# Edge messages summed by node in float32, one step later, with the message's add behind the ranks

## The chip, the cores and the metric

One core of a Trainium2 chip runs the kernel. The metric is the time of the whole program on the device in microseconds (us); the time before is the median of three runs. The profile is of one further execution. Engines are named as in the profile: PE is TensorE's matmul, PEld its weight load, DVE is VectorE, ACT ScalarE, POOL GpSimd, SP SyncE. POOL issues the indirect DMAs (gathers and scatters) in this kernel, SP most of the others.

## The reference

A message-passing step on a graph with N = 12500 nodes, E = 800000 edges, 64 features a node and 16 an edge:

```python
def reference(x, e_attr, src, dst, w_msg, w_upd):
    N, D = x.shape
    m_in = jnp.concatenate([x[src], x[dst], e_attr], axis=-1)
    msg = _silu(m_in @ w_msg)
    agg = _segment_sum(msg, dst, N)
    return _silu(jnp.concatenate([x, agg], axis=-1) @ w_upd)
```

All floating-point inputs are float32. `src` and `dst` are random, so the edges come in no order.

## The kernel before

**Tables.** At the start, x is multiplied once by the part of `w_msg` for the source (table `A_d` in DRAM, one row a node) and once by the part for the destination (table `BW` on chip, by buckets). A message is then the sum of a gathered row of `A_d`, a row of `BW` picked by a one-hot product, and the edge's 16 features times their weights.

**Sorting on chip.** Nodes are cut into 128 buckets of 98. Edges are read in chunks of 8 tiles of 128, 782 chunks in all. For a chunk, `onehot` (L362) makes the one-hot of each edge's bucket, `sums` (L368 to 371) adds these over tiles in bfloat16, `count` (L379 to 381) turns them on TensorE into each edge's rank in its bucket, `ranks` (L386) takes the largest entry, `expand` (L395 to 399) spreads each edge's record into the slot of its rank, `move` (L407) multiplies by the one-hot and so brings the records to their buckets in PSUM, ScalarE copies them to `blk` (L409), `place` (L415, 416) advances the buckets' pointers and `scatter` (L420) writes the block to the store `st` in DRAM, as one indirect DMA on POOL.

**Work list.** A group of tiles of the store (48 or 24 in two short first stages with units of u = 1 and u = 2 tiles, then 64 with units of QU = 4) is formed over several steps: `fourth` and `middle` work out on VectorE and TensorE which tiles of which bucket are complete (matmuls into `ps1` and `ps2`, read by VectorE at L512 to 514, 521 and 522), SP loads them (L497), and `fifth` takes the edges' source indices `sidx` (L463) and local destinations `lo` from them.

**Messages.** A group is worked off in batches of 8 tiles (6 in the u = 2 stage). `gather` (L574) issues one indirect DMA on POOL a tile, from `A_d` into one of three buffers `g`. `onehot` (L579) makes the one-hot `q` of the local destinations, with the edge features beside it (L580); `transpose` turns it (L588, copied to `qt` at L591), `weights` picks the bucket's rows of `BW` (L567), `product` multiplies (L597). `message` adds the gathered rows on VectorE (L603) and applies SiLU on ScalarE (L604). `parts` (L612) splits the float32 message into three bfloat16 parts by two subtractions, `reduce` multiplies them by the one-hot and so sums by node (L623; in batches with u other than 4 in float32, L625), and `add` sums the three parts (L636) and adds the result to `ACC` (L638).

**Order.** The scheduler is off: each engine gets its instructions in the order of the program text. `period()` writes out one step. It takes a chunk through one stage each of `h`, `z`, `p`, `s`, and a batch through `q` (gather and one-hot), `t` (transposes and product) and `a` (message and reduce), so that several chunks and batches are under way. After the last chunk there are periods with a batch alone, and between them `Update.run` (L878 to 886) forms the output for buckets that are done. `ends` (L901) writes terminators behind each bucket's last record.

Of the kernel before, what the change touches and what calls it, by code (L numbers as in the profile page):

```python
# [43 lines left out]
def mpnn_kernel(tc, x, e_attr, src, dst, w_msg, w_upd, out):  # L44
# [22 lines left out]
    with es:  # L67
# [62 lines left out]
        sent = cp.tile([P, 32, R], F32, name="sent")  # L130
# [69 lines left out]
        def tables():  # L200

            ts = [Nodes(qp, "q" if b0 // 4 % 2 else "qt", b0) for b0 in range(0, NB, 4)]
# [127 lines left out]
        for k in range(P // 32):  # L330
            nc.sync.dma_start(st_t[D0:D0 + DUM, k * 32 * R:(k + 1) * 32 * R], sent[0:DUM].rearrange("p a b -> p (a b)"))
# [12 lines left out]
        qp = pool("qp", 3)  # L344
# [82 lines left out]
        class Group:  # L427
# [40 lines left out]
            def fourth(g):  # L468
# [15 lines left out]
                elif k == 1:  # L484
                    a1, v, new, e0, s, e, t1, cbc = g.wl
                    g.mat = mat = wp.tile([NBK, GT], F32, name="mat")
                    nc.vector.tensor_scalar(out=mat[:, 0:gu], in0=iof[:, 0:gu], scalar1=s, scalar2=None, op0=OP.is_ge)

                    nc.vector.tensor_tensor(out=t1, in0=t1, in1=s, op=OP.subtract)
                    nc.vector.tensor_tensor(out=a1, in0=e, in1=s, op=OP.subtract)  # L490
                    nc.vector.scalar_tensor_tensor(out=mat[:, 0:gu], in0=iof[:, 0:gu], scalar=e, in1=mat[:, 0:gu], op0=OP.is_lt, op1=OP.mult)
                    nc.vector.tensor_scalar(out=cbc, in0=t1, scalar1=float(g.u), scalar2=-float(D0), op0=OP.mult, op1=OP.add)
                    nc.vector.tensor_tensor(out=g.done_new, in0=g.done_old, in1=a1, op=OP.add)
                elif k < g.t0:
                    for u in range((k - 2) * g.nl, min(gu, (k - 1) * g.nl), 8):
                        for i, t in enumerate(regs(g.row, u, min(8, gu - u), ENG.SP, TOP - g.u)):
                            j = nc.sync.dma_start(g.rt[:, (u + i) * g.u:(u + i + 1) * g.u, :].rearrange("p a c -> p (a c)"),  # L497
                                                  st_t[ds(t, g.u), :].rearrange("t (q f) -> (t q) f", f=g.u * R))
                            tc.add_to_no_dep_group("units", j.ins)
                            if len(blocks) > g.blocks:  # L500
                                for b in blocks[g.blocks:]:
                                    tc.declare_no_dep(j.ins, b, reason=WHOLE)
                                tc.add_manual_dep(j.ins, blocks[g.blocks - 1].name, mybir.DependencyInfo(mybir.DependencyClass.Sync, mybir.DependencyReason.DATA), reason=WHOLE)

            def middle(g):

                gu = g.gu
                if g.k == 0:
                    a1, v, new, e0, s, e, t1, cbc = g.wl
                    ps = pp.tile([P, 512], F32, name="ps1", tag="pl")  # L510
                    nc.tensor.matmul(ps[:, 0:1], tri, new, start=True, stop=True)
                    nc.vector.tensor_tensor(out=e0, in0=ps[:, 0:1], in1=new, op=OP.add)  # L512
                    nc.vector.tensor_scalar(out=s, in0=ps[:, 0:1], scalar1=float(gu), scalar2=None, op0=OP.min)
                    nc.vector.tensor_scalar(out=e, in0=e0, scalar1=float(gu), scalar2=None, op0=OP.min)
                elif g.k == 1:
                    cbc, mat = g.wl[7], g.mat
                    ps2 = pp.tile([P, 512], F32, name="ps2", tag="pl")
                    nc.tensor.matmul(ps2[0:1, 0:gu], cbc, mat[:, 0:gu], start=True, stop=True)
                    nc.tensor.matmul(ps2[0:1, gu:2 * gu], b64, mat[:, 0:gu], start=True, stop=True)
                    g.row, g.rb = wp.tile([1, GT], I32, name="row"), rbp.tile([1, GT], I32, name="rb")  # L520
                    nc.vector.scalar_tensor_tensor(out=g.row[:, 0:gu], in0=ps2[0:1, 0:gu], scalar=float(D0), in1=iof[0:1, 0:g.gt:g.u], op0=OP.add, op1=OP.add)
                    nc.vector.tensor_copy(g.rb[:, 0:gu], ps2[0:1, gu:2 * gu])

        class Last(Group):
# [15 lines left out]
            def middle(g):  # L540
                if g.k == 0:
                    ps = pp.tile([P, 512], F32, name="ps3", tag="pl")
                    nc.tensor.matmul(ps[0:1, 0:g.gu], g.wl[:, 1:2], ident[:, g.b0:g.b0 + g.gu], start=True, stop=True)
                    g.row = wp.tile([1, GT], I32, name="row")
                    nc.vector.tensor_copy(g.row[:, 0:g.gu], ps[0:1, 0:g.gu])

        class Batch:
# [13 lines left out]
            def weights(t):  # L561

                t.w = None
                if t.grp.u == QU:
                    t.w = qp.tile([KQ, BT // QU, D], F32, name="w")
# [16 lines left out]
            def transpose(t, step):  # L582
# [6 lines left out]
                else:  # L589
                    t.qt = qp.tile([KQ, BT * P], F32, name="qt")  # L590
# [8 lines left out]
            def message(t):  # L599
                w = t.n * D  # L600
                t.msg = mp.tile([P, 3, BT * D], F32, name="msg")
                u_ = t.msg[:, 2, :]
                nc.vector.tensor_tensor(out=u_[:, 0:w], in0=t.pre[:, 0:w], in1=t.g.rearrange("p a b -> p (a b)")[:, 0:w], op=OP.add)  # L603
                nc.scalar.activation(t.msg[:, 0, 0:w], u_[:, 0:w], AF.Silu)  # L604

            def parts(t):

                t.split = t.grp.u == QU
                if t.split:
                    up = t.msg.bitcast(BF16).rearrange("p k (f two) -> p k f two", two=2)  # L610
                    for k in range(2):
                        nc.vector.tensor_tensor(out=t.msg[:, k + 1, :], in0=t.msg[:, k, :], in1=up[:, k, :, 1], op=OP.subtract)  # L612

            def reduce(t):
                t.ag = pag.tile([P, 512], F32, name="ag")
                w = 3 * D
                if t.split:
                    q = t.q.bitcast(BF16).rearrange("p i (k two) -> p i k two", two=2)[:, :, 0:BK, 1]
                    m = t.msg.bitcast(BF16).rearrange("p k (f two) -> p k f two", two=2)[:, :, :, 1]
                for i in range(t.n):  # L620
                    u, k = i // t.grp.u, i % t.grp.u
                    if t.split:
                        nc.tensor.matmul(t.ag[0:BK, u * w:(u + 1) * w].rearrange("p (k d) -> p k d", d=D), q[:, i, :], m[:, :, i * D:(i + 1) * D], start=(k == 0), stop=(k == t.grp.u - 1))  # L623
                    else:
                        nc.tensor.matmul(t.ag[0:BK, u * D:(u + 1) * D], t.q[:, i, 0:BK], t.msg[:, 0, i * D:(i + 1) * D], start=(k == 0), stop=(k == t.grp.u - 1))  # L625

            def add(t):
# [4 lines left out]
                s = t.ag[0:BK]  # L632
                if t.split:
                    nu = BT // QU
                    s = mp.tile([BK, nu * D], F32, name="sum")
                    nc.vector.tensor_reduce(out=s.rearrange("p (u d) -> p u d", d=D), in_=t.ag[0:BK, 0:nu * 3 * D].rearrange("p (u k d) -> p u d k", k=3, d=D), axis=AX.X, op=OP.add)  # L636
                for u, a in enumerate(t.at(ACCf, ENG.DVE)):
                    nc.vector.tensor_tensor(out=a, in0=s[:, u * D:(u + 1) * D], in1=a, op=OP.add)  # L638
# [4 lines left out]
        def period(chunk=None, batch=None, ptr_new=None):  # L643

            h, z, p, s = chunk, pipe["h"], pipe["z"], pipe["p"]
            q, t, a = batch, pipe["q"], pipe["t"]
            forms = [g for g in work["forming"] if not g.ready()]
            pipe.update(h=h, z=z, p=p, q=q, t=t)
            if z:
                z.count()  # L650
            if a:
                a.message()
            if t:
                t.transpose(0)
            if h:
                h.onehot()
            if t:
                t.weights()
                t.transpose(1)
            if q:  # L660
# [5 lines left out]
            if a:  # L666
                a.parts()
# [4 lines left out]
            if z:  # L672
                z.ranks()
            for g in forms:
# [5 lines left out]
            if a:  # L680
                a.reduce()
                a.add()
            if p:
                p.place(ptr_new)
            for g in forms:
                g.middle()
                g.fifth()
            if t:
                t.product()
            return a  # L690
# [205 lines left out]
        pe = cp.tile([NBK, P // 32], I32, name="pe")  # L896

        def ends(ptr):
            for k in range(P // 32):
                nc.vector.tensor_scalar(out=pe[:, k:k + 1], in0=ptr, scalar1=float(32 * k), scalar2=None, op0=OP.add)  # L900
                i = nc.gpsimd.indirect_dma_start(out=st, out_offset=bass.IndirectOffsetOnAxis(ap=pe[:, k:k + 1], axis=0),  # L901
                                                 in_=sent.rearrange("p a b -> p (a b)"), in_offset=None)
                tc.declare_no_dep(i.ins, group="units", reason=WHOLE)
# [11 lines left out]
        def last(b=None):  # L915

            if b and b.b0 in us:
                us[b.b0].load()
# [156 lines left out]
```

## Time and profile before

| what | before |
|---|---|
| median of 3 runs | 11522.06 us (11520.64 to 11545.6) |
| the profiled execution | 11522.43 us |
| its span, first to last instruction | 11520.6 us |
| mean granted TensorE clock | 0.817 |
| busy: PE, PEld | 8812.3, 6708.3 us (76%, 58%) |
| busy: DVE, ACT, POOL | 8786.3, 2487.4, 6874.6 us (76%, 22%, 60%) |
| DMA | 521.39 MB, mean 45 GB/s |

Busy time counts instructions at work; the gap between two DMA issues on POOL is not in it. In a row of a group stand line, engine, operation, output and inputs, then the count after x, the busy time and the mean of one in ns, and the idle time of the engine just before these instructions with what ended most of it. "remote" is a semaphore whose sender the profile can't name, "issue" a time in which the engine waited for nothing that the profile shows. In a row of waits stand engine, name and line of the waiting instruction, what released it, and total, count and longest wait.

### The profile page before, as it was taken

The page shows a single profiled execution, that of the slowest core. Times are in us where ns is not written, and L with a number is a line of the kernel's source. Part 1 is how long each engine was busy: PE and PEld are TensorE (multiplying, and loading weights), DVE is VectorE, ACT ScalarE, POOL GpSimd, SP SyncE. Part 2 cuts the span into 40 slices and gives each one's busy share as a digit, 9 for nine tenths or more (in the row PEclk, how much of TensorE's full clock was granted, in tenths as well). Part 3 has the DMA queues.
Part 4 walks back from the last instruction along what each step waited for, and adds up shares of the span by engine and source line. Part 5 has one row for each costly group of instructions (what it writes and reads, how often), then busy time and mean ns, then how long its engine had stood idle before and what let it go on. Part 6 is the DMA issues. An engine that isn't in the chain of part 4 may idle for free. (4 is left out here: it accounts for less than half of the span.)

```text
span 11520.6 us, 142616 instructions
## 1 busy us (share of the span) xinstructions
PE 8812.3 (76%) x43298; PEld 6708.3 (58%) x44060; DVE 8786.3 (76%) x18300; ACT 2487.4 (22%) x5785; POOL 6874.6 (60%) x7129
## 2 busy tenths in 40 slices
PE   7777777777777777777777777777777777777566
PEld 4555555555555555655655555565655565555466
DVE  8777777888888888878888888887888888887322
ACT  2111112222222222222222222222222222222111
POOL 2455556666666666666666666666666666666555
PEclk9888888888888888788888888888888888888555
DMA  2111111111111111111111111111111111111212
GB/s 64 39 43 46 41 44 49 44 47 46 44 47 44 48 43 47 47 44 47 44 47 44 46 47 44 47 44 47 47 43 47 45 46 47 43 46 41 44 36 39
DMA packets 661675, 521.39 MB, mean 45 GB/s; under 512 B 472583, under 2 KB 520135, under 8 KB 660903
## 3 DMA queue, kind: packets, MB, share of 16 engines
q0 software_dynamic: 252672, 378.89, 12.3%
q1 hardware_dynamic: 405527, 132.58, 5.2%
q8 instruction: 359, 5.88, 0.2%
q14 instruction: 413, 3.38, 0.1%
q10 hardware_dynamic: 2704, 0.66, 0.0%
HBM read 330.05 MB, written 181.46 MB: 44 GB/s over the span
## 5 line engine op out<-in xcount | busy, mean ns | idle before, releaser
L574 POOL DMA_INDIRECT g<-A_d,sidx x6322 | 6077.2, 961 | 3146.3 <-issue 1669.5
L407 PE MATMUL pl<-X,hf 128*128 128x427 f32 (+3 forms) x12512 | 3946.6, 463 | 637.9 <-issue 463.4
L407 PEld LDWEIGHTS pl<-X,hf 128*128 128x128 f32 x12512 | 2461.8, 203 | 1966.5 <-issue 1238.1
L399 DVE TENSOR_TENSOR X<-cb,rec 128x850 f32<-128x850 f32 (+3 forms) x3128 | 2379.7, 823 | 26.8
L597 PE MATMUL pre<-w,qt 114*128 114x64 f32 x10496 | 1725.2, 333 | 458.1 <-ACT qt L591 385.0
L597 PEld LDWEIGHTS pre<-w,qt 114*128 114x128 f32 x10496 | 1653.0, 247 | 507.1 <-ACT qt L591 421.3
L604 ACT ACTIVATE msg<-msg 128x512 f32<-128x512 f32 (+1 forms) x818 | 503.3, 615 | 5688.6 <-DVE msg L603 4660.0
L603 DVE TENSOR_TENSOR msg<-pre,g 128x512 f32<-128x512 f32 (+1 forms) x818 | 550.8, 673 | 1431.6 <-remote 1041.7
L420 POOL DMA_INDIRECT st<-blk,ptrs x781 | 779.2, 998 | 1389.4 <-ACT blk L409 1099.8
L588 PE MATMUL tq<-ident,q 128*114 128x128 f32 x6322 | 1109.2, 330 | 148.5 <-issue 83.6
L588 PEld LDWEIGHTS tq<-ident,q 128*114 128x114 f32 x6322 | 988.1, 170 | 347.9 <-issue 219.5
L623 PE MATMUL ag<-msg,q 128*98 128x192 bf16 x5248 | 650.1, 268 | 581.8 <-ACT q L580 197.5
L591 ACT ACTIVATE qt<-tq 114x1024 f32<-114x1024 f32 (+1 forms) x818 | 804.9, 984 | 1283.0 <-remote 867.2
L386 DVE TENSOR_REDUCE rank<-z 128x8 f32<-128x1024 f32 x782 | 950.3, 1215 | 96.4 <-remote 69.3
L612 DVE TENSOR_TENSOR msg<-msg 128x512 f32<-128x512 f32 x1312 | 906.5, 691 | 75.5 <-issue 26.6
L623 PEld LDWEIGHTS <-q 128*98 128x98 bf16 x5248 | 542.8, 135 | 707.1 <-issue 565.0
L362 DVE TENSOR_TENSOR hf<-cb,shi 128x1024 f32<-128x1024 f32 x782 | 949.9, 1215 | 0.0
L579 DVE TENSOR_TENSOR q<-cb,lo 128x784 f32<-128x784 f32 (+1 forms) x818 | 768.4, 939 | 0.0
L409 ACT ACTIVATE blk<-pl 128x427 f32<-128x427 f32 x782 | 407.9, 522 | 1469.7 <-PE pl L407 386.2
L380 PE MATMUL z<-G,onesb 128*128 128x384 bf16 x1564 | 636.3, 407 | 115.6 <-issue 86.8
L636 DVE TENSOR_REDUCE sum<-ag 98x128 f32<-98x384 f32 x656 | 361.4, 551 | 287.2 <-remote 142.5
L379 PE MATMUL z<-hf,w 128*128 128x512 bf16 x802 | 391.5, 488 | 46.4 <-issue 27.8
(141 smaller groups left out, 6154.7 us busy)
## 6 DMA issues: line engine op xcount, KB each, us to landing
g<-A_d,sidx POOLq DMA_INDIRECT x6322
ea<-in_e_attr SPq DMA_DIRECT2D x260, 192.0 KB
rt<-st SPq DMA_DIRECT2D x1312, 34.0 KB
st<-blk,ptrs POOLq DMA_INDIRECT x781
rt<-st SPq DMA_DIRECT2D x434, 8.5 KB
nodes<-in_x SPq DMA_DIRECT2D x62, 98.0 KB
rt<-st SPq DMA_DIRECT2D x320, 17.0 KB
A_d<-nodes SPq DMA_DIRECT2D x32, 98.0 KB
```

The source lines that it names most:

```text
L362: nc.vector.tensor_tensor(out=c.hf, in0=ioB[:, None, :].to_broadcast([P, M, NBK]), in1=c.hi[:, :, None].to_broadcast([P, M, NBK]), op=OP.i ...
L386: nc.vector.tensor_reduce(out=c.rank, in_=c.z, axis=AX.X, op=OP.max)
L399: nc.vector.tensor_tensor(out=c.x[:, k:k + 2, 2:2 + n * R].rearrange("p k (s c) -> p k s c", c=R), in0=hit[:, k:k + 2, 0:n, None].to_broad ...
L407: nc.tensor.matmul(pl[:, 0:w], c.hf[:, k, :], c.x[:, k, 0:w], start=(k == M - 1), stop=(k == 0))
L420: i = nc.gpsimd.indirect_dma_start(out=st, out_offset=bass.IndirectOffsetOnAxis(ap=c.ptr, axis=0), in_=c.blk[:, 2:XR], in_offset=None)
L574: nc.gpsimd.indirect_dma_start(out=t.g[:, i, :], out_offset=None, in_=A_d, in_offset=bass.IndirectOffsetOnAxis(ap=t.grp.sidx[:, k:k + 1], ...
L579: nc.vector.tensor_tensor(out=t.q[:, 0:n, 0:BK], in0=ioB[:, None, 0:BK].to_broadcast([P, n, BK]), in1=t.grp.lo[:, i0:i0 + n, None].to_broa ...
L588: nc.tensor.transpose(t.tq[0:KQ, j * P:(j + 1) * P], t.q[:, j, :], ident)
L591: nc.scalar.activation(t.qt[:, 0:w], t.tq[0:KQ, 0:w], AF.Copy)
L597: nc.tensor.matmul(t.pre[:, i * D:(i + 1) * D], t.qt[:, i * P:(i + 1) * P], w, start=True, stop=True)
L612: nc.vector.tensor_tensor(out=t.msg[:, k + 1, :], in0=t.msg[:, k, :], in1=up[:, k, :, 1], op=OP.subtract)
L623: nc.tensor.matmul(t.ag[0:BK, u * w:(u + 1) * w].rearrange("p (k d) -> p k d", d=D), q[:, i, :], m[:, :, i * D:(i + 1) * D], start=(k == 0 ...
```

## The change

The bfloat16 split and the sum over its parts go; the reduce is a float32 matmul with 64 columns for every batch. The reduce and the add get a step of their own, `r`, one period after the message. The message's add on VectorE stands behind the ranks. In the new order TensorE gets counts, transposes, sums by node, slots, product, work list; the product is issued before the block is placed. VectorE reads the work list's matmuls a step later than they are issued. The one-hots get four buffers, `qt` and `w` a pool of their own with two. The terminators' buffer is four times as large, and one DMA takes the place of four at the start (SP) and at the end (POOL, `ends`). The bucket tables' start-up tiles and the loads in the last stage follow the new buffers and step.

The diff, cut to its core:

```diff
-        sent = cp.tile([P, 32, R], F32, name="sent")
+        sent = cp.tile([P, P, R], F32, name="sent")
...
-        for k in range(P // 32):
-            nc.sync.dma_start(st_t[D0:D0 + DUM, k * 32 * R:(k + 1) * 32 * R], sent[0:DUM].rearrange("p a b -> p (a b)"))
+        nc.sync.dma_start(st_t[D0:D0 + DUM], sent[0:DUM].rearrange("p a b -> p (a b)"))
...
-        qp = pool("qp", 3)
+        qp = pool("qp", 4)
+        qtp = pool("qtp", 2)
...
                 elif k == 1:
                     a1, v, new, e0, s, e, t1, cbc = g.wl
+                    nc.vector.tensor_tensor(out=e0, in0=g.ps[:, 0:1], in1=new, op=OP.add)
+                    nc.vector.tensor_scalar(out=s, in0=g.ps[:, 0:1], scalar1=float(gu), scalar2=None, op0=OP.min)
+                    nc.vector.tensor_scalar(out=e, in0=e0, scalar1=float(gu), scalar2=None, op0=OP.min)
...
                 elif k < g.t0:
+                    if k == 2:
+                        g.rows()
...
+            def rows(g):
+                gu = g.gu
+                g.row, g.rb = wp.tile([1, GT], I32, name="row"), rbp.tile([1, GT], I32, name="rb")
+                nc.vector.scalar_tensor_tensor(out=g.row[:, 0:gu], in0=g.ps[0:1, 0:gu], scalar=float(D0), in1=iof[0:1, 0:g.gt:g.u], op0=OP.add, op1=OP.add)
+                nc.vector.tensor_copy(g.rb[:, 0:gu], g.ps[0:1, gu:2 * gu])
...
             def message(t):
                 w = t.n * D
-                t.msg = mp.tile([P, 3, BT * D], F32, name="msg")
-                u_ = t.msg[:, 2, :]
+                u_ = mp.tile([P, BT * D], F32, name="u_")
                 nc.vector.tensor_tensor(out=u_[:, 0:w], in0=t.pre[:, 0:w], in1=t.g.rearrange("p a b -> p (a b)")[:, 0:w], op=OP.add)
-                nc.scalar.activation(t.msg[:, 0, 0:w], u_[:, 0:w], AF.Silu)
-
-            def parts(t):
...
+                t.msg = mp.tile([P, BT * D], F32, name="msg")
+                nc.scalar.activation(t.msg[:, 0:w], u_[:, 0:w], AF.Silu)
...
-                    if t.split:
-                        nc.tensor.matmul(t.ag[0:BK, u * w:(u + 1) * w].rearrange("p (k d) -> p k d", d=D), q[:, i, :], m[:, :, i * D:(i + 1) * D], start=(k == 0), stop=(k == t.grp.u - 1))
-                    else:
-                        nc.tensor.matmul(t.ag[0:BK, u * D:(u + 1) * D], t.q[:, i, 0:BK], t.msg[:, 0, i * D:(i + 1) * D], start=(k == 0), stop=(k == t.grp.u - 1))
+                    nc.tensor.matmul(t.ag[0:BK, u * D:(u + 1) * D], t.q[:, i, 0:BK], t.msg[:, i * D:(i + 1) * D], start=(k == 0), stop=(k == t.grp.u - 1))
...
-                s = t.ag[0:BK]
-                if t.split:
...
-                    nc.vector.tensor_reduce(out=s.rearrange("p (u d) -> p u d", d=D), in_=t.ag[0:BK, 0:nu * 3 * D].rearrange("p (u k d) -> p u d k", k=3, d=D), axis=AX.X, op=OP.add)
                 for u, a in enumerate(t.at(ACCf, ENG.DVE)):
-                    nc.vector.tensor_tensor(out=a, in0=s[:, u * D:(u + 1) * D], in1=a, op=OP.add)
+                    nc.vector.tensor_tensor(out=a, in0=t.ag[0:BK, u * D:(u + 1) * D], in1=a, op=OP.add)
...
         def ends(ptr):
-            for k in range(P // 32):
...
+            nc.vector.tensor_copy(pe, ptr)
+            i = nc.gpsimd.indirect_dma_start(out=st, out_offset=bass.IndirectOffsetOnAxis(ap=pe, axis=0), in_=sent.rearrange("p a b -> p (a b)"), in_offset=None)
+            tc.declare_no_dep(i.ins, group="units", reason=WHOLE)
```

The body of `period()` after the change, without its `if` lines, reads in order: `h.onehot`, `z.count`, `t.transpose(0)`, `t.weights`, `t.transpose(1)`, `r.reduce`, `q.gather` (first half), `s.scatter`, `q.gather` (second half), `h.sums`, `q.onehot`, `z.ranks`, `a.message`, `fourth`, `z.expand`, `p.move`, `t.product`, `p.place`, `r.add`, `middle`, `fifth`. Here `r` is the batch whose message was formed in the period before.

More of the change, by code (lines that the diff above doesn't have):

```diff
@@ L508, in middle @@
                 if g.k == 0:
[L509 to L514, printed above, removed]
+                    g.ps = pp.tile([P, 512], F32, name="ps1", tag="pl")
+                    nc.tensor.matmul(g.ps[:, 0:1], tri, g.wl[2], start=True, stop=True)
                 elif g.k == 1:
                     cbc, mat = g.wl[7], g.mat
[L517 to L522, printed above, removed]
+                    g.ps = pp.tile([P, 512], F32, name="ps2", tag="pl")
+                    nc.tensor.matmul(g.ps[0:1, 0:gu], cbc, mat[:, 0:gu], start=True, stop=True)
+                    nc.tensor.matmul(g.ps[0:1, gu:2 * gu], b64, mat[:, 0:gu], start=True, stop=True)
+            def rows(g):
[3 more added lines that the diff above has]
+                nc.vector.tensor_copy(g.rb[:, 0:gu], g.ps[0:1, gu:2 * gu])
         class Last(Group):
@@ L541, in middle, with rows @@
                 if g.k == 0:
[L542 to L545, printed above, removed]
+                    g.ps = pp.tile([P, 512], F32, name="ps3", tag="pl")
+                    nc.tensor.matmul(g.ps[0:1, 0:g.gu], g.wl[:, 1:2], ident[:, g.b0:g.b0 + g.gu], start=True, stop=True)
+            def rows(g):
+                g.row = wp.tile([1, GT], I32, name="row")
+                nc.vector.tensor_copy(g.row[:, 0:g.gu], g.ps[0:1, 0:g.gu])
         class Batch:
@@ L673, in period @@
                 z.ranks()
+            if a:
+                a.message()
             for g in forms:
@@ L679, in period @@
                 p.move()
-            if a:
-                a.reduce()
-                a.add()
+            if t:
+                t.product()
             if p:
                 p.place(ptr_new)
+            if r:
+                r.add()
             for g in forms:
@@ L893, in mpnn_kernel @@
         us = {b0: Update(b0) for b0 in range(0, NB, BT)}
-        pe = cp.tile([NBK, P // 32], I32, name="pe")
+        pe = cp.tile([NBK, 1], I32, name="pe")
         def ends(ptr):
-            for k in range(P // 32):
[L900 to L903, printed above, removed]
+            nc.vector.tensor_copy(pe, ptr)
+            i = nc.gpsimd.indirect_dma_start(out=st, out_offset=bass.IndirectOffsetOnAxis(ap=pe, axis=0), in_=sent.rearrange("p a b -> p (a b)"), in_offset=None)
+            tc.declare_no_dep(i.ins, group="units", reason=WHOLE)
         ends(ptrg)
```

41 lines of the change are left out of this document (13 added, 28 removed).

## The prediction

> **What bounds the kernel now.** I read the table of stages first, then the groups and waits of GpSimd (POOL) in the long stage, then one stretch of the timeline. Columns of the windows: us, then busy us of PE, PEld, DVE, ACT, POOL, the granted clock, the DMA share, GB/s.
>
> ```profile
> 0.00:1900.00 1900.00, 1472.04 (x7271) 1071.42 (x7406) 1461.56 (x3394) 364.25 (x847) 916.93 (x961) 0.88 0.19 47
> 1900.00:10450.00 8550.00, 6646.89 (x32445) 5024.30 (x33060) 6943.15 (x14003) 1922.12 (x4514) 5356.54 (x5536) 0.83 0.17 46
> 10450.00:11521.00 1071.00, 693.36 (x3584) 612.52 (x3596) 381.57 (x904) 201.01 (x424) 601.17 (x633) 0.61 0.21 41
> ```
>
> The long stage, 1900 to 10450 us, is 8550 us of the 11520.6. VectorE is busy 81% of it, TensorE 78%, POOL 63%: by busy time no engine is the bound. POOL's share misleads, as its own rows for that window show (groups, then waits as total, times, longest):
>
> ```profile
> L574 POOL DMA_INDIRECT g<-A_d,sidx x4920 | 4742.0, 964 | 2107.6 <-issue 1302.9 <-DVE msg L603 668.1 <-DMA g<-A_d,sidx 114.0
> L420 POOL DMA_INDIRECT st<-blk,ptrs x616 | 615.3, 999 | 1086.8 <-ACT blk L409 958.0 <-issue 128.2 <-DMA g<-A_d,sidx 0.3
> ...
> POOL st L420 <- ACT blk L409: 958.0, 290, 5.4
> POOL g L574 <- DVE msg L603: 668.1, 233, 5.1
> ```
>
> 616 scatters are 616 periods of one chunk and one batch, 8550/616 = 13.88 us each. POOL issues 8 gathers and one scatter in each. Busy is (4742.0 + 615.3)/616 = 8.70 us, and the gaps that follow every issue come to (1302.9 + 114.0 + 128.2)/616 = 2.51 us. So POOL needs 11.21 us of 13.88, and the rest is two kinds of pause: 958.0 us for the scatter's block (290 times, mean 3.3 us) and 668.1 us for the message's add (233 times, mean 2.87 us), together 2.64 us a period. 11.21 + 2.64 = 13.85. The floor is POOL's train of indirect DMAs, and the time above it is those pauses. Whatever moves the message or the block moves the end.
>
> Why the message is late is seen in the timeline (start, us, engine, line, and in brackets the idle time before with its releaser):
>
> ```profile
> 5006.76 1.92 PE L597 MATMUL pre<-w,qt 114*128 114x64 f32 x16
> ...
> 5008.52 0.39 PE L379 MATMUL z<-hf,w 128*128 128x512 bf16 x1
> ...
> 5009.30 0.38 PE L381 MATMUL z<-G,onesb 128*128 128x512 bf16 x1
> ...
> 5016.37 0.41 PE L407 MATMUL pl<-X,hf 128*128 128x291 f32 x1 [1.69 <-issue]
> 5016.55 0.94 POOL L574 DMA_INDIRECT g<-A_d,sidx  x1 [0.30 <-issue]
> ...
> 5019.93 0.69 DVE L603 TENSOR_TENSOR msg<-pre,g 128x512 f32<-128x512 f32 x1 [6.45 <-remote]
> 5020.54 1.22 DVE L362 TENSOR_TENSOR hf<-cb,shi 128x1024 f32<-128x1024 f32 x1
> ...
> 5020.89 0.94 POOL L574 DMA_INDIRECT g<-A_d,sidx  x1 [3.40 <-DVE msg L603]
> ```
>
> The product that the add (L603) reads ended at 5008.68, yet the add starts at 5019.93, after 6.45 us of idle VectorE. In the last part of that time the matmuls are spaced out with "issue" in front of them (1.69 us at 5016.37). The last gather ends at 5017.49, and 2.44 us later the add is let go; the next gather, which needs a gather buffer that this add frees, starts 0.96 us after the add does. TensorE's results reach the other engines late while POOL issues back to back, and arrive soon after it stops. What causes that the trace does not say; that it happens, it does.
>
> **The change part by part.** First what goes and what is resized, all on VectorE and TensorE (groups by shape: busy us, mean ns, idle us before). The whole run:
>
> ```profile
> L386 DVE TENSOR_REDUCE rank<-z 128x8 f32<-128x1024 f32 x782 | 950.3, 1215 | 96.4 <-remote 69.3 <-PE z L381 19.9 <-issue 5.8
> ...
> L362 DVE TENSOR_TENSOR hf<-cb,shi 128x1024 f32<-128x1024 f32 x782 | 949.9, 1215 | 0.0
> L612 DVE TENSOR_TENSOR msg<-msg 128x512 f32<-128x512 f32 x1312 | 906.5, 691 | 75.5 <-issue 26.6 <-ACT msg L604 19.0 <-ACT nodes L183 7.3
> ...
> L579 DVE TENSOR_TENSOR q<-cb,lo 128x784 f32<-128x784 f32 x710 | 686.7, 967 | 0.0
> ...
> L623 PE MATMUL ag<-msg,q 128*98 128x192 bf16 x5248 | 650.1, 268 | 581.8 <-ACT q L580 197.5 <-DVE msg L612 154.5 <-issue 145.2
> ...
> L636 DVE TENSOR_REDUCE sum<-ag 98x128 f32<-98x384 f32 x656 | 361.4, 551 | 287.2 <-remote 142.5 <-PE tq L588 64.2 <-PE pre L597 36.1
> L370 DVE TENSOR_TENSOR G<-G,hf 128x256 bf16<-128x256 bf16 x782 | 352.7, 451 | 26.7
> ...
> L370 DVE TENSOR_TENSOR G<-hf 128x256 bf16<-128x256 f32 x782 | 327.8, 419 | 5.1
> ...
> L371 DVE TENSOR_TENSOR G<-G,hf 128x128 bf16<-128x128 bf16 x782 | 228.5, 292 | 26.9
> ```
>
> and, between 300 and 1200 us, where the reduce is in float32 already:
>
> ```profile
> L625 PE MATMUL ag<-msg,q 128*98 128x64 f32 x824 | 82.5, 251 | 5.3 <-ACT msg L604 5.2
> ```
>
> *Split and its sum go.* Two subtractions (L612) and one reduce (L636) for each of 656 batches: (906.5 + 361.4)/656 = 1.93 us of VectorE a batch, 1268 us in all. VectorE falls from 81% to about 67% of the long stage. I cost this at nothing, because the train of POOL covers it; if VectorE were the bound it would be worth up to 616 x 1.93 = 1190 us, and rivals C and D are what it would buy.
>
> *The reduce becomes float32.* The rows give 650.1/5248 = 0.124 us a tile in bfloat16 with 192 columns. A float32 matmul leaves two records, so L625 has 824/2 = 412 tiles at 82.5/412 = 0.200 us. Eight tiles cost 8 x 0.076 = 0.61 us more TensorE a batch, 400 us over 656. Its cover is TensorE's 22% idle time; without it the 400 us would be paid. I take nothing.
>
> *The reduce and the add go one step later.* They then read a message that has been ready for most of a period, so TensorE no longer stands at the reduce with the product queued behind it. In the long stage the train covers this; in the last stage it doesn't (below). The extra q and qt buffers only keep operands alive for that step.
>
> *The message goes behind the ranks.* This is the term that counts. Behind the add wait SiLU on ScalarE, then the reduce, and on POOL the first gather of the batch after next, since three gather buffers rotate and the add frees one; the scatter stands behind four of those gathers. In its new place the add runs after the one-hot (L362), the sums, q's one-hot (L579) and the ranks (L386), and the ranks wait for TensorE's counts. In a pause VectorE will mostly have done the first three and stand at the ranks instead of at the message. Once TensorE's results arrive, the ranks run first: 1.215 us. The counts come directly behind the product on TensorE, from 5008.52 to 5009.68, so they can be later than the product by their own 1.16 us. Price of a message pause: from +1.2 to +2.4 us. I take 1.5, near the lower row, as the counts ended 10 us before the release in the stretch shown. A gain is possible as well, when the freed 1.93 us lets the add be early enough that POOL never stops: that is rival C. 233 x 1.5 = +350 us. The block's 290 pauses keep their price: slots are moved behind the expansion in both orders.
>
> By the Trainium skill, page "SBUF — State Buffer", section "SBUF: two separate sides", only VectorE and GpSimd share a port pair, and TensorE never waits on anyone there. By that rule the 6.45 us could not come from the gathers, the message would be released with its product, and the 668.1 us could fall to nothing, which is what rival C's chance stands for. The row at 5016.37 with 1.69 us of "issue" inside a POOL train speaks against it.
>
> *The work list is read a step later.* In the second stage (u = 2) each group of 24 tiles has one long period. The rows from 400 to 1750 us:
>
> ```profile
> POOL g L574 <- DVE sidx L463: 252.8, 26, 12.5
> ...
> POOL g L574 <- DVE msg L603: 138.2, 43, 3.9
> ...
> DVE row L521 <- remote: 80.1, 22, 5.3
> DVE ACC L638 <- remote: 62.9, 16, 7.8
> ```
>
> The 80.1 and 62.9 us of VectorE's waits for the list's matmuls and for the same period's reduce vanish, since both are now read in the next step. POOL feels them through the 252.8 us that it waits for a new group's indices. Against that, the tile loads (SP's queue) start later in their step, because their row numbers are written behind ranks and message, and 43 message pauses cost 1.5 us more, +65. Ends: -143 if all of the waits were POOL's, +65 if none. About half of -143 against +65: I take 0.
>
> *The last stage.* From about 10450 no chunk is left, so neither ranks nor counts stand ahead of the message. POOL from 10500 to 11300, and a stretch of the timeline:
>
> ```profile
> POOL g L574 <- DVE msg L603: 161.1, 47, 11.1
> ...
> 11000.55 2.81 PE L625 MATMUL ag<-msg,q 128*98 128x64 f32 x16
> ...
> 11003.16 3.62 PE L597 MATMUL pre<-BW,qt 114*128 x16
> ...
> 11007.82 0.94 POOL L574 DMA_INDIRECT g<-A_d,sidx  x1 [0.30 <-issue]
> 11011.62 0.68 DVE L603 TENSOR_TENSOR msg<-pre,g 128x512 f32<-128x512 f32 x1
> ...
> 11012.57 0.94 POOL L574 DMA_INDIRECT g<-A_d,sidx  x1 [3.81 <-DVE msg L603]
> ```
>
> Each product (11003.16) stands behind a reduce (11000.55, 2.81 us at the low clock) that waits for the message before. With the reduce a step later the product can start that much earlier, and 47 pauses shrink by up to 2.81 us: -132 us, bounded above by 0 (the release still comes late) and below by -161. I take -120.
>
> *Four DMAs become one* for the terminators, at the start and at the end:
>
> ```profile
> L901 POOL DMA_INDIRECT st<-sent,pe x4 | 4.2, 1054 | 15.7 <-issue 10.4 <-DMA st<-sent,pe 2.8 <-DVE ACC L638 2.6
> ```
>
> Four issues and their gaps are 19.9 us; three go, so -15 at most, and 0 if the larger one takes as long. I take -10. The store at the start lies under the other loads: 0.
>
> Sum, on the profiled execution's 11522.4 us (span 11520.6 and 1.8 around it; the median of the runs shown is 0.4 below it): +350 + 0 - 120 - 10 = +220, so 11,742; I say 11,740 us. With the ends of its terms (280 to 560 on pauses, -143 to +65, -161 to 0, -15 to 0) it could be 11,483 to 12,147. Not all ends meet: its own range is 11,560 to 12,000.
>
> **The rivals.**
> *B: the message caught behind a whole period.* Same mechanism, larger: where VectorE still stands at the block's place or the add when TensorE's results arrive, the message also has the one-hot 1.215, sums 1.16 (L370 twice and L371) and q's 0.97 in front of it, which with the ranks' 1.215 and the counts' 1.16 makes 5.7 us. It decides if the pause begins before VectorE has ended its period. At half of 233: 116 x 5.7 + 117 x 1.5 = 837, less 130, gives 12,230 us. For it: only three gather buffers tie POOL to the add. Against: VectorE has 1.93 us more slack.
>
> *C: the slack removes the message's pauses.* VectorE, at 67%, is always ahead, the product has several us more to arrive, and POOL never stops for the message. -668 if all go; the scatter's pauses would take some over, since TensorE's results still only come when POOL stops. Half: -334 - 130 = 11,058 us; all: 10,724. For it: VectorE's freed time and the product's extra time. Against: the ranks need TensorE just as the message did.
>
> *D: TensorE's late results go altogether* with the shorter chain, and POOL runs at its floor: -(958.0 + 668.1) - 130 = 9,766 us. Against: 290 pauses hang on the slot blocks, whose path is not shortened.
>
> *No change*: losses in the long stage meet gains in the last, as at the low ends of the sum.
>
> **How the numbers follow.** The forecast (A) gets 0.40, B 0.22, C 0.26, D 0.08, no change 0.04. Two tenths of a per cent, 23 us, is about what this kernel's runs can tell from nothing. Faster is C + D = 0.34, the same 0.04, slower A + B = 0.62. The range takes in C down to 10,900 and B up to 12,350, leaving out D, the deeper part of C and the worst of B, together about 0.19. On its own the slower side is 11,560 to 12,350.
>
> **What would show it.** Right: the period between scatters grows from 13.88 to some 14.4 us; the message's pauses on POOL stay near 233 but rise from 2.87 to above 4 us each; VectorE's long "remote" waits move from the message to the ranks and VectorE falls under 70%; the reduce costs TensorE about 0.6 us more a batch; message pauses after 10450 shrink. Wrong: if POOL's pauses for the message fall well below 668 us, C or D holds and the lateness is not tied to POOL as I read it; if the ranks don't wait and the time still grows, TensorE or the list is the cause.

## The result and the profile after

The changed kernel took 11,641.62 us (median of 4 runs, 11,629.23 to 11,649.94) beside 11,525.28 us for the kernel before: a ratio of 1.0097, 95% interval 1.0079 to 1.0114. That is slower by 1%, about half of the 1.9% forecast and inside the range. The profiled execution's span is 11,643.4 us, 122.8 us more than before.

Where those 122.8 us lie is found with POOL's gathers, of which both kernels issue 6322 in the same order. Taking the start of the 1st, 801st, 5501st, 5801st and last from the two traces gives five stretches and what is left at the end (us):

| stretch | before | after | difference | forecast |
|---|---|---|---|---|
| start to gather 1 | 232 | 244 | +12 | 0 |
| gathers 1 to 801 (u = 1, u = 2) | 1692 | 1743 | +51 | 0 |
| gathers 801 to 5501 (chunk and batch) | 8166 | 8196 | +30 | +350 |
| 5501 to 5801 (chunks end) | 521 | 520 | -1 | 0 |
| 5801 to 6322 (batches alone, terminators) | 867 | 893 | +27 | -130 |
| last gather to the end | 44 | 47 | +3 | 0 |

The total was near and the parts were not. The table of stages of the changed kernel (us, busy us of PE, PEld, DVE, ACT, POOL, granted clock, DMA share, GB/s):

```profile
0.00:1900.00 1900.00, 1429.88 (x7041) 1030.08 (x7172) 1406.13 (x3276) 369.28 (x816) 878.78 (x918) 0.86 0.18 45
1900.00:10450.00 8550.00, 6862.13 (x37241) 5289.03 (x37853) 5806.09 (x12114) 1941.99 (x4496) 5319.38 (x5517) 0.87 0.17 46
```

VectorE falls from 6943 to 5806 us in the long stage, 81% to 68%, as costed, and the stage hardly notices. POOL's groups and its longest waits there:

```profile
L580 POOL DMA_INDIRECT g<-A_d,sidx x4904 | 4705.7, 960 | 1898.4 <-issue 1455.1 <-DVE wl L488 115.1 <-DVE wl L479 78.4
L420 POOL DMA_INDIRECT st<-blk,ptrs x613 | 614.0, 1002 | 1332.2 <-ACT blk L409 1240.1 <-issue 83.9 <-ACT w L573 4.1
...
POOL st L420 <- ACT blk L409: 1240.1, 448, 5.4
```

613 scatters in the window make 13.95 us a period, against 13.88. The gathers' idle time that is neither issue nor a DMA (23.8 us) is 1898.4 - 1455.1 - 23.8 = 420 us; before it was 2107.6 - 1302.9 - 114.0 = 691. The scatter's wait for its block went the other way, 958 us in 290 pauses to 1240 us in 448. Together that is 1649 and 1660 us: the pauses moved from the message to the block. That their sum stayed says no more than that the period did, since POOL's busy time and its short gaps changed little. One stretch of the changed kernel's timeline shows the stall behind this:

```profile
5015.39 1.14 PE L616 MATMUL ag<-msg,q 128*98 128x64 f32 x11 [0.31 <-issue]
...
5017.81 0.22 PE L616 MATMUL ag<-msg,q 128*98 128x64 f32 x1 [1.28 <-issue]
...
5018.54 0.22 PE L616 MATMUL ag<-msg,q 128*98 128x64 f32 x1 [0.51 <-issue]
...
5020.94 0.95 POOL L580 DMA_INDIRECT g<-A_d,sidx  x1 [0.30 <-issue]
5022.07 0.26 PE L616 MATMUL ag<-msg,q 128*98 128x64 f32 x1 [1.03 <-issue]
5022.79 6.89 PE L407 MATMUL pl<-X,hf 128*128 128x427 f32 x16 [0.46 <-issue]
5024.27 1.22 DVE L386 TENSOR_REDUCE rank<-z 128x8 f32<-128x1024 f32 x1 [5.76 <-remote]
...
5025.41 0.68 DVE L608 TENSOR_TENSOR u__39204<-pre,g 128x512 f32<-128x512 f32 x1
...
5026.36 0.95 POOL L580 DMA_INDIRECT g<-A_d,sidx  x1 [4.47 <-DVE wl L479]
```

Here the ranks wait 5.76 us for counts, the message's add (L608 now) runs behind them, and POOL stands for 4.47 us: the pause that was forecast, in the place where it was forecast. Between 5017 and 5022 the reduce's records come 0.7 or 1.4 us apart with "issue" ahead of them; in the period before (5005.48) all 16 of them took 1.57 us. TensorE's groups for 1900 to 10450 us show how much that is, first before, then after:

```profile
L407 PE MATMUL pl<-X,hf 128*128 128x427 f32 (+3 forms) x9840 | 3087.9, 461 | 418.3 <-issue 391.3 <-DVE LOST L415 6.6 <-DVE ptrs L416 5.7
```

```profile
L407 PE MATMUL pl<-X,hf 128*128 128x427 f32 (+3 forms) x9808 | 3236.7, 484 | 397.1 <-issue 212.3 <-DVE rank L386 103.8 <-DVE wl L487 36.2
L603 PE MATMUL pre<-w,qt 114*128 114x64 f32 x9808 | 1384.8, 287 | 564.3 <-issue 531.4 <-ACT msg L610 21.7 <-ACT G L368 6.0
L616 PE MATMUL ag<-msg,q 128*98 128x64 f32 x9808 | 1083.7, 261 | 524.5 <-issue 336.3 <-DVE ACC L624 128.7 <-ACT qt L597 26.0
```

In the changed kernel these three groups alone have 1080 us of "issue". TensorE's busy time and that come to 6862 + 1080 = 7942 of 8550 us, 93%, so by this sum TensorE is nearly the bound there.

### The profile page after: what moved, and what is told of

It reads as the page before. It is cut to its first block, busy times and chain, and to the rows that moved or that the text cites. A ratio compares the mean times of both kernels' runs of the same rounds, so it can differ in the third digit from the quotient of the medians.

```text
span 11643.4 us, 151057 instructions
## 1 busy us (share of the span) xinstructions
PE 9063.1 (78%) x48547; PEld 7005.0 (60%) x49308; DVE 7595.1 (65%) x16329; ACT 2534.7 (22%) x5785; POOL 6854.8 (59%) x7126
## 5 line engine op out<-in xcount | busy, mean ns | idle before, releaser
L407 PE MATMUL pl<-X,hf 128*128 128x427 f32 (+3 forms) x12512 | 4183.4, 490 | 629.6 <-issue 222.5
L407 PEld LDWEIGHTS pl<-X,hf 128*128 128x128 f32 x12512 | 2564.4, 211 | 2040.2 <-issue 1146.7
L616 PE MATMUL ag<-msg,q 128*98 128x64 f32 x12644 | 1447.2, 267 | 731.6 <-issue 423.3
L603 PE MATMUL pre<-w,qt 114*128 114x64 f32 x10496 | 1491.8, 289 | 587.5 <-issue 553.0
L616 PEld LDWEIGHTS ag<-msg,q 128*98 128x98 f32 x12644 | 1374.3, 185 | 827.2 <-issue 616.6
L603 PEld LDWEIGHTS pre<-w,qt 114*128 114x128 f32 x10496 | 1463.6, 209 | 657.8 <-issue 620.9
L415 DVE SCALAR_TENSOR_TENSOR LOST<-blk 128x1 f32<-128x1 f32 x782 | 123.1, 157 | 2308.0 <-ACT blk L409 2149.5
L624 DVE TENSOR_TENSOR ACC<-ag,ACC 98x64 f32 x1938 | 435.2, 225 | 826.6 <-issue 350.8
L603 PE MATMUL pre<-BW,qt 114*128 (+1 forms) x2148 | 320.6, 311 | 130.1 <-ACT qt L597 59.1
L368 ACT ACTIVATE G<-hf 128x256 bf16<-128x256 f32 x782 | 321.2, 411 | 374.0 <-DVE hf L362 309.8
L603 PEld LDWEIGHTS pre<-BW,qt 114*128 114x128 f32 x2148 | 319.2, 228 | 134.3 <-ACT qt L597 76.5
```

The costliest lines, as they stand in the source:

```text
L407: nc.tensor.matmul(pl[:, 0:w], c.hf[:, k, :], c.x[:, k, 0:w], start=(k == M - 1), stop=(k == 0))
L603: nc.tensor.matmul(t.pre[:, i * D:(i + 1) * D], t.qt[:, i * P:(i + 1) * P], w, start=True, stop=True)
```

## The experiments

The experiments ran on three chips (labels e, f and g, one chip each), each beside the kernel before. There that kernel took 9,574, 9,577 and 9,581 us (medians), not 11,522, so ratios and stretches are compared, not times across the two. Which chip ran the pair above isn't on record; it is called the recorded chip here. The stretches are those of the table above. The expectations weigh theories by a letter: P is the prediction's price of the message's place, T has TensorE as the bound, L has POOL stop for TensorE's late results in any order, and G has the work list's later step delay each group. The profile of the kernel before comes first, since everything else is read against it.

**The kernel before, unchanged.**

> The kernel before, for its profile beside the others. Without TensorE's stalls: time 9,570 us; G expects gathers 0 to 800 in about 1,340 us as in e4, so that the list's later step is a loss against it, and gathers 800 to 5500 some 150 to 250 us above the 6,690 of the changed kernel, which is what VectorE's freed time is worth there.

It took 9,587 us in one run, with 1341 us for the first 800 gathers and 6872 for the next 4700, as expected. POOL and one TensorE group from 2000 to 8500 us, and the window's busy times:

```profile
L574 POOL DMA_INDIRECT g<-A_d,sidx x4445 | 4296.4, 967 | 1395.2 <-issue 1179.6 <-DMA g<-A_d,sidx 104.0 <-DVE msg L603 84.2
...
L407 PE MATMUL pl<-X,hf 128*128 128x359 f32 (+3 forms) x8892 | 2580.8, 443 | 31.4 <-DVE rb L522 25.3 <-DVE wl L513 5.6
...
2000.00:8500.00 6500.00, 5577.28 (x29845) 4219.87 (x29843) 6249.40 (x12630) 1696.17 (x4069) 4851.52 (x5000) 0.90 0.22 54
```

The slot matmuls (L407) show no "issue" time; on the recorded chip they had 391 us. POOL's wait for the message is 84 us in 555 periods instead of 668 in 616. A period is 11.71 us instead of 13.88, and now VectorE is the busiest engine, 6249.4 of 6500 us, 96%. The stalls belong to the chip or its circumstances, not to the kernel alone. POOL issues more densely here than on the recorded chip, so its train alone does not make TensorE late either. A low granted clock alone doesn't do it: the mean clock was 0.817 and 0.845 in the recorded pair and 0.884 here, but e3 below ran at 0.836, and in its long stage no matmul starts more than 0.3 us after the end of the one before it in its group. On the recorded chip the changed kernel has 793 such matmuls between 2000 and 8500 us.

**The changed kernel, again.**

> The changed kernel itself, beside the ones to compare with it. Theory G (group formation): the new order's loss sits in the u = 2 stage, where each group's indices come later; theory L as before: TensorE's results come late while POOL issues, on some chips. Where the stalled TensorE records (0.7 us apart) are absent, G expects the ratio to the kernel before at 1.00 to 1.02, with POOL at its floor after 2000 us and 250 to 320 us more than in e4 for gathers 0 to 800; where they are present, 1.008 to 1.012 again.

It took 9,649 us, ratio 1.0075 (1.0059 to 1.0092), as G expected without stalls: nearly the same 1%, by another path. The stretches, from the profile of each run:

| kernel | to 1 | 1-801 | 801-5501 | 5501-5801 | 5801-6322 | end | ratio |
|---|---|---|---|---|---|---|---|
| before (g1) | 235 | 1341 | 6872 | 437 | 675 | 26 | 1 |
| changed (f1) | 240 | 1614 | 6696 | 427 | 656 | 23 | 1.0075 |
| changed, list undone (f2) | 235 | 1407 | 6686 | 426 | 656 | 23 | 0.9839 |
| changed, rows undone (g2) | 238 | 1509 | 6679 | 425 | 654 | 26 | 0.9960 |
| changed, message in front (e1) | 241 | 1652 | 6674 | 425 | 654 | 28 | 1.0107 |
| before, float32 reduce (e4) | 232 | 1339 | 6682 | 425 | 665 | 23 | 0.9789 |
| before, message behind (e3) | 232 | 1325 | 7754 | 494 | 753 | 47 | 1.1085 |

The change wins 176 us in the long stage and loses 273 in the first two. POOL's gathers in the long stage of f1 (2000 to 8500 us):

```profile
L580 POOL DMA_INDIRECT g<-A_d,sidx x4564 | 4362.9, 956 | 1391.8 <-issue 1007.6 <-DMA g<-A_d,sidx 282.6 <-DVE rank L386 21.7
L420 POOL DMA_INDIRECT st<-blk,ptrs x570 | 572.6, 1005 | 173.8 <-issue 131.1 <-ACT msg L610 13.4 <-ACT w L573 7.0
```

The pauses for message and block are gone: 6500/570 = 11.40 us a period, and (4362.9 + 572.6 + 1391.8 + 173.8)/570 = 11.41. The train of indirect DMAs is the whole of it.

**A longer train.** To see whether POOL really sets the end there:

```diff
             if s:
+                for _ in range(4):
+                    nc.gpsimd.memset(idle_t, 0.0)
                 s.scatter()
```

> The changed kernel with four fills of 512 columns on POOL ahead of each scatter, an idle stretch of one to three us that computes nothing. If POOL's train is the floor, the time grows by 781 times the length of the stretch less what falls into its waits in the first stage: +800 to +2,000 us. Where TensorE's stalls are present and pauses are forced by them (L), the stretch takes the place of a forced pause: less than +300 us.

It took 11,121 us in one run, 1,472 above f1, as expected if the train is the floor. The fills, in the page's groups:

```profile
L651 POOL MEMSET idle_t<- 128x512 f32 x3128 | 1658.5, 530 | 135.2
```

Four of them are 4 x (1658.5 + 135.2)/3128 = 2.29 us. Gathers 801 to 5501 hold 587.5 periods, so 1347 us are expected if each is paid in full; the stretch went from 6696 to 8042, +1346. Between gathers 1 and 801, where 132 scatters would have cost 303 us, the time rose by 24: there POOL waits for something else. With no stalls present, the other case of the expectation could not be tried.

**The list read in the same step again.**

```diff
     elif k == 1:
-        nc.vector.tensor_tensor(out=e0, in0=g.ps[:, 0:1], in1=new, op=OP.add)
...
-        if k == 2:
-            g.rows()
...
         nc.tensor.matmul(g.ps[:, 0:1], tri, g.wl[2], start=True, stop=True)
+        nc.vector.tensor_tensor(out=e0, in0=g.ps[:, 0:1], in1=new, op=OP.add)
...
         nc.tensor.matmul(g.ps[0:1, gu:2 * gu], b64, mat[:, 0:gu], start=True, stop=True)
+        g.rows()
```

> The changed kernel with the work list read in the same step again (the three operations after ps1, and row and rb after ps2, back where they were). If the later list alone makes the groups late: 200 to 300 us below f1 without TensorE's stalls, 20 to 80 below with them. If the order of reduce, product and place does it: within 40 us of f1.

It took 9,423 us, ratio 0.9839 (0.9823 to 0.9855): 226 us below f1, as expected of the list alone, and in the two profiles 207 of the difference lie in gathers 1 to 801. So the list's later step alone turns a gain of 1.6% into a loss. TensorE's waits from 240 to 1600 us, f1 and then f2:

```profile
PE pl L407 <- DVE wl L487: 127.9, 27, 8.6
PE pl L407 <- DVE rb L526: 84.6, 27, 4.0
```

```profile
PE ag L617 <- DVE ACC L625: 144.6, 91, 2.5
PE ag L617 <- DVE rec L258: 19.5, 14, 2.0
...
PE pl L407 <- DVE wl L513: 3.4, 1, 3.4
```

In f1 the slot matmuls wait 127.9 + 84.6 = 212.5 us, 27 times each, once per group of 24 tiles, for VectorE's reads of the list. In f2 that is 3.4 us. Why a slot matmul waits for the list is in the code: `ps1`, `ps2` and `pl` have the same tag in a PSUM pool (`pp`) of one buffer. While the list's result sits there until the next step, the next slots can't start. A stretch of f1:

```profile
785.78 1.22 DVE L386 TENSOR_REDUCE rank<-z 128x8 f32<-128x1024 f32 x1
786.91 0.55 DVE L608 TENSOR_TENSOR u__6489<-pre,g 128x384 f32<-128x384 f32 x1
787.38 0.15 DVE L486 TENSOR_TENSOR wl<-ps,wl 128x1 f32<-128x1 f32 x1
787.44 0.15 DVE L487 TENSOR_SCALAR wl<-ps 128x1 f32<-128x1 f32 x1
...
787.64 7.46 PE L407 MATMUL pl<-X,hf 128*128 128x427 f32 x16 [4.54 <-DVE wl L487]
...
795.13 0.53 ACT L409 ACTIVATE blk<-pl 128x427 f32<-128x427 f32 x1 [7.06 <-PE pl L407]
795.69 0.16 DVE L415 SCALAR_TENSOR_TENSOR LOST<-blk 128x1 f32<-128x1 f32 x1 [3.96 <-ACT blk L409]
```

The reads stand behind ranks and message on VectorE; the slots start 0.2 us after the second of them, after 4.54 us of idle TensorE, and take 7.46 us at a mean granted clock of 0.62, where the slots at 772.38 took 4.60 at 1.00. VectorE then waits 3.96 us for their block. The four periods of a group, scatter to scatter, have means of 8.9, 12.8, 11.7 and 16.3 us in f1 (600 to 1500 us) and 9.0, 8.9, 8.9 and 15.7 in f2. Not all of the 207 us need be waits: the mean granted clock over gathers 1 to 801 is 0.88 in f1 and 0.96 in f2, and TensorE is busy there for 1265 and 1205 us.

**Half of the list.** Only `row` and `rb` are put back behind `ps2`; the three operations after `ps1` stay a step later.

> The changed kernel with only the second half of the list's move undone (row and rb right after ps2; the three operations after ps1 stay a step later). Rows theory: the tile loads wait for row, so this gives most of f2's 226 us: 9,430 to 9,480 us. Otherwise, if the operations after ps1 or VectorE's waits in the same step make it, less than half: above 9,540 us.

It took 9,540 us, ratio 0.9960 (0.9945 to 0.9974). The expectation that `row` gives most of it because the tile loads wait for it missed: gathers 1 to 801 take 1509 us, 105 below f1, and the other 102 belong to the operations after `ps1`, which no load waits for directly. In its trace from 240 to 1600 us the slots' wait for `rb` is gone and the one for the read at L487 stands at 137.9 us. Two holds of one PSUM buffer, each about half, is what fits. A list with a PSUM buffer of its own, which would show it directly, was not run.

**The message's add in front again.** The call of `a.message()` moves from behind `z.ranks()` to the head of the period.

> The changed kernel with the message's add back at the head of VectorE's step, all else as changed. Three theories. P (the prediction's): the add's place behind the ranks costs 1.5 us at some 233 pauses, so this takes about 350 us off the changed kernel's 11,642: about 11,300 us. T (TensorE): with VectorE freed, TensorE paces the long stage (busy plus issue gaps are 94% of it in the changed kernel, 86% before), the add's place is nearly free: 11,600 to 11,680 us. L (late hand-over): POOL has to stop about once a period for TensorE's results whatever stands first in line: 11,600 to 11,680 us as well.

It took 9,677 us, ratio 1.0107 (1.0090 to 1.0124): nothing is gained, where theory P promised 3%. The same move on top of f2, in one group with it:

> f2 with the message's add at the head of VectorE's step as well. G: within 40 us of f2. P (the add's place costs 1.5 us at each pause): 300 us below f2 where TensorE's stalls are present.

It took 9,478 us, 55 us above f2 (ratio 0.9898, 0.9882 to 0.9915) and outside G's 40. The place behind the ranks is the better one by 0.6% on this chip, so the sign that theory P gives to the move is wrong there; in the profiles 37 us of the difference lie in gathers 1 to 801. For a chip with stalls this was not measured.

**The reduce in bfloat16** (upper halves of the messages alone):

```diff
+                q = t.q.bitcast(BF16).rearrange("p i (k two) -> p i k two", two=2)[:, :, 0:BK, 1]
+                m = t.msg.bitcast(BF16).rearrange("p (f two) -> p f two", two=2)[:, :, 1]
...
-                    nc.tensor.matmul(t.ag[0:BK, u * D:(u + 1) * D], t.q[:, i, 0:BK], t.msg[:, i * D:(i + 1) * D], start=(k == 0), stop=(k == t.grp.u - 1))
+                    nc.tensor.matmul(t.ag[0:BK, u * D:(u + 1) * D], q[:, i, :], m[:, i * D:(i + 1) * D], start=(k == 0), stop=(k == t.grp.u - 1))
```

> The changed kernel with the reduce in bfloat16 on the upper half of each message alone (the lower bits of the messages are left out of the sums): 8 instead of 16 matmul records a batch, VectorE and order unchanged. T: about 0.8 us less TensorE a period at full clock and half the stalled instructions, so 500 to 700 us off: about 11,050 us. P: the reduce is covered, 11,640 us within 40. L: pauses forced by POOL's trains stay, 11,640 us within 40.

It took 9,646 us, ratio 1.0077 (1.0060 to 1.0094), the same as f1. The float32 reduce is covered where TensorE doesn't stall, and theory T falls for these chips.

**Float32 in the old order.** In the kernel before, `t.split = False`: no split, no sum over parts, reduce in float32, nothing moved.

> The kernel before without the split and the sum over its parts, reduce in float32 in the same step, order and buffers as before. P: VectorE's 1268 us were covered and so is the reduce: 11,520 us within 40, a little faster. T: TensorE has 0.6 to 0.8 us more a period, of which VectorE's shorter path gives part back: 11,550 to 11,800 us. L: 11,520 us within 40.

> e4 again, beside the changed kernel: the kernel before without split and sum, reduce in float32. Without TensorE's stalls 0.979 of the kernel before again. With them, L: within 0.5% of the kernel before, since POOL's pauses are set by the late results and not by VectorE; T (TensorE is the bound there): 1 to 3% above it.

The two runs took 9,370 and 9,375 us, ratios 0.9789 (0.9772 to 0.9805) and 0.9790 (0.9773 to 0.9806): faster than both kernels, by one line. None of the first run's three theories expected a gain beyond 40 us; the second run's expectation was made with the first one known. Gathers 801 to 5501 are at POOL's floor (6682 us) and gathers 1 to 801 as short as before (1339). All that the change had to give, but for the terminators, is in this line; the new order adds nothing to it here.

**The message behind the ranks in the old order**, with the split behind the expansion and the reduce in the same step:

> The kernel before with the message's add moved behind the ranks and the split behind the expansion, nothing else. P: +1.5 us at 233 pauses and more, since the split and the reduce follow in the same step: 11,850 to 12,100 us. T: TensorE stands at the reduce for a late message, +0.5 us a period or so: 11,700 to 11,900 us. L: pauses only change their place: 11,520 us within 60.

It took 10,609 us, ratio 1.1085 (1.1067 to 1.1104), above every expectation (at most 12,100 of 11,522, 1.05). TensorE from 1500 to 8500 us:

```profile
PE ag L623 <- DVE msg L612: 1207.1, 442, 5.8
```

It stands at the reduce 442 times for a message that was only just split, with the product queued behind. In the change, where the split is gone and the reduce comes a step later, the same place is cheap. Which of the two makes it so, this run can't tell.

**The gains together.** e4 with one DMA for the terminators:

> e4 with the terminators' one DMA for four at the start and the end. The parts that gained, put together: 10 to 20 us below e4, 9,355 to 9,370 us, 0.977 to 0.978 of the kernel before.

It took 9,381 us, ratio 0.9790 (0.9774 to 0.9806), no better than e4, so the 10 to 20 us expected don't show. The stretch 5801 to 6322 fell from 665 to 656 us, so the end's three DMAs are worth about 9 us, less than these totals can tell.

## Why the prediction was right or wrong

**The total was right for reasons that were not.** +218 us were forecast and 116 measured, slower as said. But +350 for the long stage was +30, and what was costed at 0 (up to gather 801) and -130 (from gather 5801) came to +63 and +27. That these add up to the right side is luck.

**The message's pause (+1.5 us at 233 pauses): the step that failed.** The mechanism can be seen (5024.27: ranks wait, message behind, POOL stands), but the gathers' waits other than issue and DMAs, nearly all of them for the message, fell from 691 to 420 us instead of rising. By the prediction's own sign of being wrong, message pauses well below 668 us speak for rival C, the freed VectorE time, and rival C's caveat came with it: the scatter's pauses took the gain over (448 in place of 290). The prediction took the pauses one by one and held the block's 290 fixed. The two traces show one kind growing by 282 us as the other shrinks by 271. The reading that fits is that POOL stops at one place or the other where TensorE hands over late, and a later message only decides which. It was not tried, since no experiment met the stalls, and the 93% of TensorE leave open that TensorE itself holds the period.

**"What causes it the trace does not say".** The tie of the stalls to POOL's train was read from one chip. On the three chips of the experiments POOL runs denser trains and TensorE has no "issue" time worth the name (at L407 at most 0.5 of 31.4 us in g1, against 391.3 of 418.3). By the Trainium skill, page "SBUF — State Buffer", section "SBUF: two separate sides", TensorE never waits for GpSimd's port; those three chips agree with it. What stalls TensorE on the recorded one, and why before and after are 20% slower there, stays open. One thing more can be read from the trace of the changed kernel: of the 1024 matmuls between 1900 and 10450 us that start over 0.3 us late behind one of their own group, 662 do so within the 6 us ahead of a fall of the granted clock from 1 to 0.5, in stretches that make up 26% of that time. f1 has 153 such falls between 1900 and 8500 us and no such matmul, so the falls don't explain the stalls; the two only come together.

**VectorE's 1.93 us at nothing.** The recorded chip doesn't contradict it (13.88 and 13.95 us a period with VectorE at 81% and 68%, though other parts changed as well). Elsewhere it is wrong: there VectorE was 96% busy and its relief is worth 11.71 - 11.40 = 0.31 us a period, 176 us. That is near rival D's floor, 11.21 us worked out and 11.40 measured, on chips where the late results that D wanted gone are absent from the start.

**The float32 reduce at nothing.** Right without stalls (e2: no difference). Its size was low: 0.61 us a batch were worked out, and the long stage's rows give 1083.7/613 - 601.0/616 = 0.79 us. On the recorded chip TensorE came to 93% with its stalled records, and whether half the records would have helped there wasn't measured.

**The list a step later at 0: the second step that failed.** The prediction weighed VectorE's waits against later tile loads and missed what the list's matmuls are written into. Undoing the later step is worth 226 us (f2) and makes the changed kernel faster than the one before, so on that chip this step alone decides that the change is slower. That it acts through the one PSUM buffer which the list shares with the slots fits the 212.5 us of waits and the code. On the recorded chip the first two stretches lost 63 us. The same wait is there, as the group from 400 to 1750 us of the changed kernel's first profile shows, but the kernel before was already at 1692 us in place of 1341, and how much of the 63 us it makes was not measured:

```profile
L407 PE MATMUL pl<-X,hf 128*128 128x427 f32 (+3 forms) x1647 | 596.4, 523 | 172.0 <-DVE wl L487 98.9 <-DVE rb L526 50.7 <-DVE wl L486 22.0
```

**The last stage (-120) and the terminators (-10).** The reduce no longer holds the product up: before it waited 90.3 us for SiLU between 10500 and 11300 us, and after no such wait is among its longest. But without stalls POOL has no pauses to win there (675 to 656 us, half of it the terminators), and on the recorded chip POOL's waits for VectorE from gather 5801 on rose from 195 to 226 us, fewer and longer ones. Why they did isn't shown. -10 for the terminators is what g4 shows by its stretch, -9.

## What to carry to other kernels

Before reading a result a step later "for free", look at which buffer holds it in the meantime and who needs that buffer next. An engine that is off the bound can be relieved with no loss, but the gain is only as large as its distance to the next bound (here 0.31 us of VectorE over POOL's 11.40). When several waits end the same train, cost their sum, not each by itself: one that is removed may come back at the next. And undo each part of a change alone: on these chips a single line of this one is worth 2.1%, and the rest takes it back.

## What was not expected of the hardware

The same kernel took 11,522 us in the recorded pair and 9,574 to 9,581 us on the three chips of the experiments. The difference shows as TensorE records 0.7 us apart with nothing to wait for, and as results that arrive at other engines microseconds late (6.45 us at the message before, 5.76 at the ranks after); a gather's own duration is the same on both (964 and 967 ns). And work put into the 0.3 us gap ahead of a scatter is not hidden by it: 2.29 us of fills there cost 1346 us over 587.5 periods, 2.29 us each.
